# An attention-and-state-space kernel whose instruction order is planned: choosing the plan by replays, loading x's last block by column chunks, and moving two GpSimd steps

## The chip, the cores and the metric

The kernel runs on one NeuronCore of a Trainium2 chip. The metric is device time in microseconds (us) of one execution, as the median of several runs; lower is better. Engines in the text: PE (TensorE, matrix products), ACT (ScalarE), DVE (VectorE), POOL (GpSimd) and SP (SyncE, which here only issues DMAs).

## What is computed

Two independent halves, joined along the last axis: a state-space layer on `A_x` and multi-query attention on `B_x`, both with 2048 rows and 640 columns.

```python
def _A_ref(x, Lambda_re, Lambda_im, B_re, B_im, C_re, C_im, log_dt, Dskip):
    Lam_bar = exp(exp(log_dt) * Lam)                      # complex, 640 states
    Bu = einsum("bld,pd->blp", x, ((Lam_bar - 1) / Lam)[:, None] * Bmat)
    h[t] = Lam_bar * h[t-1] + Bu[t]                       # 2048 steps
    return 2 * einsum("blp,dp->bld", h, Cmat).real + x * Dskip

def _B_ref(x, wq, wk, wv, wo):                            # 32 heads of 20, one key and value head
    q, k, v = x @ wq, x @ wk, x @ wv
    p = softmax(q @ k.T * 20 ** -0.5)                     # 32 x 2048 x 2048
    return (p @ v).reshape(2048, 640) @ wo
```

## The kernel before

**Attention sets the length.** Scores are made transposed, in tiles of 128 keys by 512 queries: 4 blocks of queries x 8 groups of 4 heads x 16 key blocks x 4 heads = 2048 tiles. PE makes a tile (`score`, lines "SC<-QT,KT"); its exponential is taken either by ACT (`fill`, L1417: one ACTIVATE for two or three tiles of a PSUM slot, "PR<-SC") or by DVE, which forms the bits of a bf16 exponential by integer arithmetic (`fill_d`, L816, "BIG<-SC 128x512") and then needs three shifted copies of the result. POOL makes those copies two tiles at a time (`copy`, L1732, INT64_ADD) or DVE does (L816, "BIG<-BIG"). PE multiplies the exponentials with the values ("MB<-PR,VP" and, for DVE's tiles, four products each, "MB<-BIG,VS"), 32 query-head blocks one after the other, each ended by a copy of its PSUM bank (L1799, "pvsb"). There are two PSUM slots of three banks, SC0 and SC1, which ACT reads in turn.

**Beside it** PE, DVE and SP carry the rest as tasks: the projections of q (L1239, sent through DRAM as `qd` and brought back as `QT` by SP), the products of the state-space layer ("xaT", "CT,W", "CA,W"), the scaling of its matrices (`scale_b`, `scale_c`: L815, L816 and L811, "CA<-BA,sc", "W<-CT,sc"), the output projection.

**The prologue.** x (`B_x`) comes in four blocks of 512 rows. Blocks 0 and 1 are loaded as they lie and turned on PE (`turn`, with the identity `ident`, which DVE clears and POOL completes, L929); blocks 2 and 3 come through a transposing DMA (`loads`, L664): block 3 in two halves of 256 rows by 640 columns (`XB`). For each block `kv` (L1074 on) multiplies the five column chunks with `wkr` into one PSUM bank ("SC<-BIG,wkr"), takes the absolute maximum on DVE (L1087, `mab`) and writes the keys `KT` (L1093 on ACT; for block 1 on DVE). For block 3 it does so in two parts of 256 columns in the same bank. `bound` makes a bound from the maxima (L1113 to L1124: `Mp`, then `M0`), `qt_task` multiplies `M0` into the first query block, DVE writes it ("QT<-MB,lift"), and only then can the first score tile be made.

**What sets the order.** Each kernel instruction is an `Op` with an engine, a planned duration and dependences. `Schedule.run` plays a list-scheduling plan with those planned durations: on each engine, whenever it is free, `pick` takes the ready operation with the lowest `prio` whose `gate` holds. A DMA's planned landing comes from its bytes, its `issue` and `land` numbers, or from a fixed `lands`. `planned` (L509) makes 24 plans, the first with the task list as it stands and the others with due times moved by up to 12 tiles at random, and keeps the one with the earliest planned end. `Emitter.plan` then turns that plan into one fixed stream per engine with semaphore waits. On the chip each engine runs its stream in order: an instruction that waits holds all that is behind it. Waits are found per name: all columns of a PSUM bank carry one name, so a read of one half also waits for a write of the other half that stands ahead in the plan.

`keep_source` (L885) puts four 256-column products that change nothing ("MB<-KT,VZ", the left operand is zero) into PE's stream where the plan has had little matrix work in the last 3 us (`KEEP`).

## Time and profile before

| | us |
|---|---|
| median of 3 runs (all: 715.91, 712.63, 715.94) | 715.91 |
| the profiled execution | 715.61 |
| its span, first to last instruction | 713.9 |
| PE busy | 690.2 |
| ACT busy | 692.5 |
| DVE busy | 618.3 |
| POOL busy | 458.6 |
| first exponential of ACT starts | 20.35 |

The time outside the span (715.61 - 713.9 = 1.7 us) is launch and end. Times in the views are counted from the span's start. A row of a timeline gives the start, the length (of several merged instructions if "x" is above 1), the engine and the operation as output<-input; the bracket at its end is the idle time of the engine ahead of it and what ended it.

### The profile page before, as it was taken

The page shows a single profiled execution, that of the slowest core. Times are in us where ns is not written, and L with a number is a line of the kernel's source. Part 1 is how long each engine was busy: PE and PEld are TensorE (multiplying, and loading weights), DVE is VectorE, ACT ScalarE, POOL GpSimd, SP SyncE. Part 2 cuts the span into 40 slices and gives each one's busy share as a digit, 9 for nine tenths or more (in the row PEclk, how much of TensorE's full clock was granted, in tenths as well). Part 3 has the DMA queues.
Part 4 walks back from the last instruction along what each step waited for, and adds up shares of the span by engine and source line. Part 5 has one row for each costly group of instructions (what it writes and reads, how often), then busy time and mean ns, then how long its engine had stood idle before and what let it go on. Part 6 is the DMA issues. An engine that isn't in the chain of part 4 may idle for free.

```text
span 713.9 us, 26755 instructions
## 1 busy us (share of the span) xinstructions
PE 690.2 (97%) x11256; PEld 246.1 (34%) x11257; DVE 618.3 (87%) x1193; ACT 692.5 (97%) x700; POOL 458.6 (64%) x777
## 2 busy tenths in 40 slices
PE   7999989999999999999999999999999999999997
PEld 3322232343333433333433233334333333343323
DVE  7899869988998888788889999899999998877794
ACT  6899989999999999999999999999999999999996
POOL 3247745015688677565857867687767777868790
PEclk9999999999999999999999999999999999999999
DMA  9677642111111001101301001130000010110001
GB/s 187 171 176 165 141 92 67 45 30 25 32 45 31 13 19 25 48 16 30 65 7 39 19 11 39 34 68 15 13 19 20 11 25 26 27 38 18 25 14 40
DMA packets 77589, 34.44 MB, mean 48 GB/s; under 512 B 58350, under 2 KB 77470, under 8 KB 77470
## 3 DMA queue, kind: packets, MB, share of 16 engines
q1 hardware_dynamic: 76506, 32.44, 19.4%
q8 instruction: 90, 1.47, 0.9%
q10 hardware_dynamic: 964, 0.29, 0.2%
q14 instruction: 29, 0.24, 0.1%
HBM read 11.53 MB, written 9.75 MB: 30 GB/s over the span
## 4 chain that ended last, share of the span: by engine, by line
ACT 48%; PE 45%; SPq 2%; DMA 2%; DVE 2%; issue 1%; DVEq 0%
ACT PR L1417 48%; PE MB L679 17%; PE SC L679 11%; PE MB L749 11%; PE MB L759 4%; DMA CT<-in_A_C_im_dram 1%; SPq L664 1%; DMA BIG<-in_B_x_dram 1%; DVE BIG L816 1%; PE MB L675 1%; SPq L1851 1%; PE SC L749 0%; PE SC L675 0%; SPq L1291 0%; SPq L660 0%
## 5 line engine op out<-in xcount | busy, mean ns | idle before, releaser
L1417 ACT ACTIVATE PR<-SC 128x1024 bf16<-128x1024 f32 (+1 forms) x679 | 679.0, 1199 | 7.5 <-PE SC L679 5.2
L1732 POOL INT64_ADD BIG<-BIG x743 | 446.8, 618 | 224.9 <-DVE BIG L816 116.6
L816 DVE TENSOR_SCALAR BIG<-SC 128x512 int16<-128x512 f32 x531 | 357.3, 685 | 63.7 <-PE SC L679 58.2
L679 PE MATMUL SC<-QT,KT 32*128 32x512 bf16 x2014 | 266.1, 385 | 12.2 <-ACT PR L1417 5.8
L679 PE MATMUL MB<-BIG,VS 128*32 128x512 bf16 x2260 | 251.1, 384 | 0.5 <-DVE pvsb L1799 0.5
L679 PE MATMUL MB<-PR,VP 128*32 128x512 bf16 x1483 | 212.3, 384 | 0.4 <-DVE pvsb L1799 0.4
L679 PEld LDWEIGHTS SC<-QT,KT 32*128 32x128 bf16 x2014 | 67.8, 91 | 187.5 <-ACT PR L1417 125.0
L679 PEld LDWEIGHTS MB<-BIG,VS 128*32 128x32 bf16 x2260 | 60.1, 95 | 63.5 <-issue 41.9
L679 PEld LDWEIGHTS MB<-PR,VP 128*32 128x32 bf16 x1483 | 50.6, 94 | 48.9 <-issue 36.7
L749 PE MATMUL MB<-CT,W 128*32 128x320 bf16 (+2 forms) x1004 | 53.5, 301 | 0.2
L816 DVE TENSOR_SCALAR BIG<-BIG 128x1024 int16<-128x1024 int16 (+1 forms) x112 | 41.6, 404 | 2.8 <-PE MB L679 1.9
L749 PE MATMUL MB<-CA,W 128*32 128x512 bf16 (+1 forms) x640 | 35.4, 302 | 0.1
L759 PE MATMUL MB<-xaT,BT 32*128 32x256 bf16 x168 | 32.8, 275 | 1.1 <-ACT PR L1417 1.1
L749 PE MATMUL MB<-xaT,BA 128*32 128x256 bf16 x800 | 33.3, 280 | 0.6 <-DVE BIG L1239 0.6
L759 PE MATMUL MB<-diagD,xaT 32*128 32x128 bf16 x320 | 31.4, 217 | 0.0
L749 PEld LDWEIGHTS MB<-CT,W 128*32 128x32 bf16 x1004 | 22.8, 96 | 15.4 <-issue 6.8
L759 PEld LDWEIGHTS MB<-diagD,xaT 32*128 32x128 bf16 x320 | 17.7, 92 | 28.8 <-ACT PR L1417 20.9
L1984 DVE CAST stg<-MB 128x512 bf16<-128x512 f32 x35 | 23.8, 680 | 4.4 <-PE MB L749 3.6
L749 PE MATMUL MB<-xaT,BT 128*32 128x256 bf16 x632 | 26.6, 276 | 0.0
L811 DVE TENSOR_TENSOR prod<-MB,tab 128x1024 bf16<-128x1024 f32 x20 | 24.3, 1213 | 1.4 <-PE SC L679 1.0
L816 DVE TENSOR_SCALAR BIG<-MB 128x512 int16<-128x512 f32 x34 | 23.1, 679 | 0.0
L2251 DVE TENSOR_TENSOR_SCAN g<-sc,hst,prod 128x256 bf16<-128x256 f32 x30 | 22.9, 779 | 0.1
(168 smaller groups left out, 461.0 us busy)
## 6 DMA issues: line engine op xcount, KB each, us to landing
out_dram<-stg SPq DMA_DIRECT2D x31, 128.0 KB, 1.9
qd<-BIG SPq DMA_DIRECT2D x20, 128.0 KB, 2.2
QT<-qd SPq DMA_DIRECT2D x28, 80.0 KB
OP<-pvsb SPq DMA_DIRECT2D x105, 20.0 KB
rdP<-recs SPq DMA_DIRECT2D x105, 20.0 KB
lbd<-BA SPq DMA_DIRECT2D x5, 320.0 KB, 3.0
CT<-in_B_x_dram SPq DMA_DIRECT2D x2, 640.0 KB, 5.2
BA<-in_A_B_re_dram SPq DMA_DIRECT2D x1, 800.0 KB, 7.1
```

What stands on the lines that cost most here:

```text
L664: fns = [lambda e, o=o, i=i: e.dma_start_transpose(o, i) for o, i in pairs]
L675: r = e.matmul(out[32 * j:32 * j + 32], lhsT=lhsT[:, 32 * j:32 * j + 32], rhs=rhs, start=start, stop=stop, tile_position=(0, 32 * j), skip ...
L679: return lambda e: e.matmul(out, lhsT=lhsT, rhs=rhs, start=start, stop=stop, **kw)
L749: x = e.matmul(out[32 * j:32 * j + 32], lhsT=lhsT[:, 32 * j:32 * j + 32], rhs=rhs, start=start, stop=r.end is tag, tile_position=(0, 32 * ...
L759: return lambda e: e.matmul(out, lhsT=lhsT[at], rhs=rhs[at], start=False, stop=r.end is tag, tile_position=(32 * row, 0), skip_group_check ...
L811: return lambda e: e.tensor_tensor(out, a, b, op)
L816: return lambda e: e.tensor_scalar(out, a, s1, s2, op0=op0, op1=op1)
L1417: ex = self.act(lambda e: e.activation(dst, t[:, 0:512 * n], ACT.Exp, scale=1.0 / UNIT), 0.8333 * 512 * n + 64, table="exp", deps=[op], re ...
L1732: op.fns.append(lambda e: e.int64_add(words(dst), words(src), add))
L1851: fns = [lambda e, j=j, d=d, to=to, n=n, at=at: e.dma_start(p.OP[to:to + n, at, :], p.pvsb[32 * j + d:32 * j + d + n, slot, :]) for j, d, ...
L1984: ev = self.dve(lambda e: e.tensor_copy(st, bank.ap), 645, deps=[prev], reads=[bank.key], writes=[key], prio=self.EV, gate=(lambda: last.e ...
L2251: o = self.dve(lambda e, ri=ri, init=init: e.tensor_tensor_scan(p.g[:, u, ri, :], rdec, p.prod[:, 1, 0, ri, :], init, ALU.mult, ALU.add), ...
```

## The change

- `planned` makes 32 plans. Of each whose planned end lies within `MARGIN` of the best so far it also makes the streams, and `replay` runs those streams 12 times with other landing times for the DMAs (a mean and a spread for each kind, `FLIGHTS`, and now and then a late one). The plan with the lowest mean end is kept. `MARGIN = 2000.0` stands behind `planned`, but the class sets `MARGIN = 650.0` again further down (it did so before, for `fill_now`), so 650 ns is what counts.
- x's block 3 is transposed in two chunks of columns, 512 rows by 384 and 512 rows by 256. `kv` multiplies and reduces each block in one part of 512 columns, so `mab` has four maxima and `bound` one step less. All four `KT` are written by ACT.
- POOL's `ident` step has a lower `prio` number than its other constants, and POOL steps of more than 600 ns (that is the clearing of `VS`, 128x2048) wait in the plan until the first `mab` has started.
- Planned numbers change: `LANDS`, a table `LAND` of added flight time for DMAs (2500 ns for the transposes of B and C, `bt` and `ct`, in place of 1000 and 0; 1500 for `ba`; 2000 for `bn`), `KEEP` 3500 to 4200, `KEEP_Q` 4 in place of 12, `LATER` 5 in place of 7, 1850 for the clearing of `VS`.

```diff
-        for seed in range(self.PLANS):                     # PLANS = 24
+        for seed in range(self.PLANS):                     # PLANS, REPLAYS = 32, 12
...
-            end = max(op.end for op in plan.s.order) + self.COLD * self.quiet(plan.s.order)
+            cold = self.COLD * self.quiet(plan.s.order)
+            if best is not None and max(op.end for op in plan.s.order) + cold > best[0] + self.MARGIN:
+                continue
+            em = Emitter(self.nc, plan.s.order, [b.key for b in plan.banks], self.shared())
+            em.plan()
+            end = sum(em.replay(random.Random(k)) for k in range(self.REPLAYS)) / self.REPLAYS + cold
             if best is None or end < best[0]:
-                best = (end, plan)
+                best = (end, em)
...
+    def replay(self, rng):
+        S = Schedule
+        free, end = dict.fromkeys(S.ENGINES, 0.0), {}
+        for op in self.order:
+            e = op.eng
+            t = free[e]
+            for o in self.waits_of[id(op)]:
+                lag = S.OUT["dma"] if o.dma_key is not None else S.OWN.get(e, 0.0) if o.eng == e else S.OUT[o.eng]
+                t = max(t, end[id(o)] + lag)
+            if op.dma_key is not None:
+                free[e] = t + op.tail * len(op.fns)
+                if op.lands is not None:
+                    end[id(op)] = max(t + 1500.0, op.lands + abs(rng.gauss(0.0, 300.0)))
+                    continue
+                planned = op.end - op.start
+                mean, spread = self.FLIGHTS.get(op.dma_key.rstrip("0123456789"), (planned - 1000.0 * (planned > 3500.0), 500.0))
+                late = rng.gauss(mean, spread) + (rng.expovariate(1.0 / 1500.0) if rng.random() < 0.03 else 0.0)
+                end[id(op)] = t + max(1500.0, late)
+            else:
+                end[id(op)] = t + op.dur + op.tail
+                free[e] = t + op.dur - (S.EARLIER.get(e, 0.0) if op.psum else 0.0)
+        return max(end.values())
...
-    KEEP = 3500.0
+    KEEP, KEEP_Q = 4200.0, 4
...
-                                  prio=1 if eng == "pool" else 0.7, port=eng == "pool")
+                                  prio=(0.5 if name == "ident" else 1) if eng == "pool" else 0.7, port=eng == "pool",
+                                  gate=(lambda: 0 in self.red_op and self.red_op[0].start is not None) if dur > 600 and eng == "pool" else None)
...
-            o = self.loadT([(p.xbT[:, :, 512 * tb + lo:512 * tb + hi], xb[0, 512 * tb + lo:512 * tb + hi, :])], 800 * (hi - lo),
-                           f"xb{tb}{lo}", issue=6.0 * (hi - lo), writes=[f"xbT{tb}_{c}" + "h" * (lo > 0) for c in range(NC)])
+            o = self.loadT([(p.xbT[:, lo:hi, 512 * tb:512 * tb + 512], xb[0, 512 * tb:512 * tb + 512, 128 * lo:128 * hi])], 78000 * (hi - lo),
+                           f"xb{tb}{lo}", issue=600.0 * (hi - lo), writes=[f"xbT{tb}_{c}" for c in range(lo, hi)])
...
-    TURNED, KEYS = ("dadad", "dadad"), "adaa"
-    XB = ((2, 0, 512, 11100.0), (3, 0, 256, 12200.0), (3, 256, 512, 13100.0))
+    TURNED, KEYS = ("dadad", "dadad"), "aaaa"
+    XB = ((2, 0, 5, 11250.0), (3, 0, 3, 12500.0), (3, 3, 5, 13400.0))
+    LAND = dict(xa=1500.0, xa2=2000.0, bn=2000.0, bt=2500.0, ct=2500.0, ba=1500.0, pc=1200.0, qd=300.0)
...
-            parts = len(self.xb_op[tb, 0])
-            n = 512 // parts
-            for x in range(parts):
-                for c in range(NC):
-                    prev = self.pe(self.four(bank, [p.wkr[:, c, :]] * 4, p.xbT[:, c, 512 * tb + n * x:512 * tb + n * x + n],
-                                             c == 0, c == NC - 1, n * x, n), self.mmt(n), mode="C", prio=self.KP if tb < 3 else 1.15,
-                                   deps=[self.xb_op[tb, c][x], self.wk_op] + bank.last, prev=prev,
-                                   reads=[self.x_keys(tb, c)[x], "wkr"], writes=[bank.key])
-                red = self.dve(lambda e, src=bank.cols(n * x, n * x + n), at=tb + x: e.tensor_reduce(
-                    out=p.mab[:, at:at + 1], in_=src, axis=AX.X, op=ALU.max, apply_absolute_value=True), 115 + 1.05 * n, deps=[prev],
+            for c in range(NC):
+                prev = self.pe(self.four(bank, [p.wkr[:, c, :]] * 4, p.xbT[:, c, 512 * tb:512 * tb + 512], c == 0, c == NC - 1),
+                               self.mmt(512), mode="C", prio=self.KP if tb < 3 else 1.15,
+                               deps=[self.xb_op[tb, c], self.wk_op] + bank.last, prev=prev,
+                               reads=[f"xbT{tb}_{c}", "wkr"], writes=[bank.key])
+            red = self.dve(lambda e, src=bank.ap: e.tensor_reduce(out=p.mab[:, tb:tb + 1], in_=src, axis=AX.X, op=ALU.max,
+                                                     apply_absolute_value=True), 650, deps=[prev], reads=[bank.key],
...
-    EARLIER, LATER = 4, 7
+    EARLIER, LATER = 4, 5
```

Because the order is planned, nearly every stream changes. Counted in the streams of the two built kernels:

| | before | after |
|---|---|---|
| ACT exponentials of 1024 / 1536 / 512 columns | 554 / 125 / 0 | 557 / 123 / 1 |
| DVE exponentials (128x512) | 565 | 564 |
| shifted copies on DVE (one tile / two tiles) | 15 / 97 | 14 / 77 |
| shifted copies on POOL | 743 | 762 |
| zero products "MB<-KT,VZ" of 256 columns | 96 | 148 |
| DVE exponentials ahead of the first "W<-CT,sc" (L816; L862 in the new kernel) | 49 | 54 |
| products with the values that stand behind the last wait for an exponential of ACT | 13 | 4 |

More of the change, by code (lines that the diff above doesn't have):

```diff
@@ L114, in done @@
     def done(self, ops):
-        return all(o.end is not None and o.end + self.OUT.get(o.eng, 60.0) <= self.t for o in ops)
+        t = self.t
+        for o in ops:
+            if o.clear > t:
+                return False
+        return True
     def ready(self, op):
@@ L889, in keep_source @@
             return None
-        if self.pv_filled[b] == 64 and sum(len(q) for q in self.pvq[b]) < 12:
+        if self.pv_filled[b] == 64 and sum(len(q) for q in self.pvq[b]) < self.KEEP_Q:
             return None
@@ L1040, in xa_load @@
         self.xa_op[tb] = [self.loadT([(p.xaT[:, :, eo, lo:lo + 256], self.every(self.A_x[0, 512 * tb:512 * tb + 512, :], eo))], 327680,
-                                     f"xa{eo}", issue=1450.0, writes=[f"xaT{tb % 2}_{c}_{eo}" for c in range(NC)]) for eo in range(2)]
+                                     f"xa{eo}", issue=1450.0, land=self.LAND["xa2"], writes=[f"xaT{tb % 2}_{c}_{eo}" for c in range(NC)]) for eo in range(2)]
     @staticmethod
@@ L1074, in kv @@
         def kv(tb):
-            yield lambda: all((tb, c) in self.xb_op for c in range(NC)) and (tb < self.PLAIN or self.s.done(self.xb_op[tb, 0][:1])) \
+            yield lambda: all((tb, c) in self.xb_op for c in range(NC)) and (tb < self.PLAIN or self.s.done([self.xb_op[tb, 0]])) \
                 and any(x in self.early for x in self.free_banks)
@@ L1150, in v_task @@
                             for i in (2 * h, 2 * h + 1) for c in range(NC)], 10 * 28.0, mode="F", load=200.0,
-                           deps=[o for c in range(NC) for o in self.xb_op[tb, c]] + [self.wv_op] + bank.last, prev=prev, prio=3 if tb < 2 else 0.97,
-                           reads=[k for c in range(NC) for k in self.x_keys(tb, c)] + ["wvr"], writes=[bank.key],
+                           deps=[self.xb_op[tb, c] for c in range(NC)] + [self.wv_op] + bank.last, prev=prev, prio=3 if tb < 2 else 0.97,
+                           reads=[f"xbT{tb}_{c}" for c in range(NC)] + ["wvr"], writes=[bank.key],
                            gate=lambda: self.lively(self.V_BY[tb // 3]))
@@ L1184, with four @@
     started = False
-    def four(self, bank, lhs, rhs, start, stop, at=0, n=512):
-        return [self.mm(bank.tensor[32 * j:32 * j + lhs[j].shape[-1], bank.off + at:bank.off + at + n], lhs[j], rhs, start, stop,
+    def four(self, bank, lhs, rhs, start, stop):
+        return [self.mm(bank.tensor[32 * j:32 * j + lhs[j].shape[-1], bank.off:bank.off + 512], lhs[j], rhs, start, stop,
                         tile_position=(0, 32 * j), skip_group_check=True) for j in range(4)]
```

103 lines of the change are left out of this document (53 added, 50 removed).

## Prediction

> **What bounds the kernel now.** The page comes first: which engine is full, and which one the chain that ended last runs through.
>
> ```profile
> span 713.9 us, 26755 instructions
> PE 690.2 (97%) x11256; PEld 246.1 (34%) x11257; DVE 618.3 (87%) x1193; ACT 692.5 (97%) x700; POOL 458.6 (64%) x777
> ACT 48%; PE 45%; SPq 2%; DMA 2%; DVE 2%; issue 1%; DVEq 0%
> L1417 ACT ACTIVATE PR<-SC 128x1024 bf16<-128x1024 f32 (+1 forms) x679 | 679.0, 1199 | 7.5 <-PE SC L679 5.2
> ```
>
> ACT's 679 exponentials are busy for 679.0 us, 1.00 us each with their overlap. The timelines of ACT give their frame: start, last group, and the copy that follows them.
>
> ```profile
> 20.35 28.95 ACT L1417 ACTIVATE PR<-SC 128x1024 bf16<-128x1024 f32 x31 [1.58 <-PE SC L679]
> 689.59 15.60 ACT L1417 ACTIVATE PR<-SC 128x1024 bf16<-128x1024 f32 x14
> 706.34 0.60 ACT L1804 ACTIVATE pvsb<-MB 128x512 bf16<-128x512 f32 x1 [1.14 <-PE MB L679]
> ```
>
> They run from 20.35 to 689.59 + 15.60 = 705.19. So the profiled 715.61 us are a prologue of 20.35, 684.84 of exponentials of which 684.84 - 679.0 = 5.84 is idle, a tail of 713.9 - 705.19 = 8.7, and 1.7 outside the span. The profiled execution lies 0.3 below the median of 715.91. Whatever PE, DVE or POOL save counts only where it shortens one of these four pieces.
>
> Where are the 5.84? In one place, most of them:
>
> ```profile
> 100.19 1.02 ACT L1417 ACTIVATE PR<-SC 128x1024 bf16<-128x1024 f32 x1 [1.46 <-PE SC L679]
> 102.31 1.02 ACT L1417 ACTIVATE PR<-SC 128x1024 bf16<-128x1024 f32 x1 [1.10 <-PE SC L679]
> 103.84 1.02 ACT L1417 ACTIVATE PR<-SC 128x1024 bf16<-128x1024 f32 x1 [0.50 <-PE SC L679]
> 105.20 1.45 ACT L1417 ACTIVATE PR<-SC 128x1536 bf16<-128x1536 f32 x1 [0.33 <-PE SC L679]
> ```
>
> 1.46 + 1.10 + 0.50 + 0.33 = 3.39 us. The timelines of SP, DVE and PE, and the windows (length, then busy us and counts of PE, PEld, DVE, ACT and POOL, clock, DMA share, GB/s), say why:
>
> ```profile
> 66.78 3.69 SPq L664 DMA_TRANSPOSE CT<-in_A_C_re_dram  x1
> 91.58 3.28 SPq L664 DMA_TRANSPOSE CT<-in_A_C_im_dram  x1
> 91.84 0.68 DVE L816 TENSOR_SCALAR BIG<-SC 128x512 int16<-128x512 f32 x1
> 94.58 0.33 DVE L1840 RECIPROCAL rc<-dn 64x32 bf16<-64x32 bf16 x1
> 98.46 0.55 DVE L816 TENSOR_SCALAR W<-CT,sc 128x1280 bf16<-128x1280 bf16 x1 [3.54 <-DMA CT<-in_A_C_im_dram]
> 99.76 0.39 PE L679 MATMUL SC<-QT,KT 32*128 32x512 bf16 x3 [1.82 <-DVE BIG L816]
> 100.73 0.96 PE L749 MATMUL MB<-xaT,BA 128*32 128x256 bf16 x20 [0.57 <-DVE BIG L1239]
> 99.00:100.00 1.00, 0.24 (x3) 0.13 (x3) 1.00 (x4) 0.00 (x0) 0.00 (x0) 1.00 0.06 7
> 101.00:102.00 1.00, 1.00 (x25) 0.33 (x13) 1.00 (x3) 0.22 (x1) 0.95 (x2) 0.54 0.09 21
> 103.00:104.00 1.00, 1.00 (x17) 0.38 (x17) 0.17 (x2) 0.50 (x2) 0.59 (x2) 0.50 0.22 48
> ```
>
> DVE reaches the first step of `scale_c` at 94.92 and stands for 3.54 us, because the transposed C_im, issued at 91.58, lands only at 98.46. The DVE exponential behind it holds a PSUM slot, so PE cannot refill it (1.82 us idle), ACT runs dry (1.46), and right after that PE's granted clock is 0.50 for about three us, in which ACT loses the other 1.93. Everything is late because one DVE instruction stands too early in its stream.
>
> **The change, part by part.**
>
> *The C_im wait.* In the new streams the first `W<-CT` stands behind 54 DVE exponentials, not 49. The 49th is scored together with ACT's 74th exponential, the new 54th with ACT's 80th: 6 later at 1.00 us. The 49th ended at 92.52, so the new 54th ends about 92.5 + 6.0 - 0.6 (the shorter prologue, below) = 97.9, and `W<-CT` follows it at once. SP issues from 66.78 to 91.58 with pauses of 0.1 us or less; the new order has the same 25 issues there, in another order, and one `qd` store (0.45 us in the row below) less ahead of them. So C_im is issued at about 91.6 - 0.6 - 0.45 = 90.5 and lands 98.46 - 91.58 = 6.88 later, at 97.4, half a us before DVE asks.
>
> ```profile
> 83.77 0.45 SPq L1241 DMA_DIRECT2D qd<-BIG  x1
> ```
>
> That is thin. SP now has to pass the `brow` loads, which wait for a DVE step that stood behind the 35th DVE exponential and now stands behind the 43rd; by the same count it is done at about 85 us, when SP arrives. If SP waits up to 2 us there, DVE waits up to 1.5 at C_im. I take 0.5 us of wait left, with no fall of the clock: 3.39 - 0.5 = **2.9 us gained**; bounds 2.0 and 3.4.
>
> *x's block 3.* The rows of the prologue (PE, DVE), and the two sizes of the reduction by form:
>
> ```profile
> 16.12 0.40 PE L679 MATMUL SC<-BIG,wkr 128*32 128x256 bf16 x8 [0.56 <-DMA BIG<-in_B_x_dram]
> 16.58 0.42 DVE L1087 TENSOR_REDUCE mab<-SC 128x1 f32<-128x256 f32 x1 [2.26 <-PE SC L679]
> 17.06 0.51 PE L679 MATMUL SC<-BIG,wkr 128*32 128x256 bf16 x12 [0.53 <-DVE mab L1087]
> 17.62 0.42 DVE L1087 TENSOR_REDUCE mab<-SC 128x1 f32<-128x256 f32 x1 [0.23 <-PE SC L679]
> 18.16 0.35 DVE L1121 SCALAR_TENSOR_TENSOR M<-mask,mab,Mp 128x128 bf16<-128x128 f32 x1
> 18.60 0.40 PE L679 MATMUL MB<-BIG,M 128*32 128x512 bf16 x4
> L1087 DVE TENSOR_REDUCE mab<-SC 128x1 f32<-128x512 f32 x3 | 2.0, 683 | 0.0
> 707.10 0.60 PE L675 MATMUL SC<-WO,OP 128*32 128x512 bf16 x8
> ```
>
> The last half lands at 16.08 (PE starts 0.04 later). Its products are cut in two by the first half's reduction: that stands behind 8 of them because the bank has one name, and the other 12 stand behind it. From landing to the `M0` product: 18.60 - 16.08 = 2.52 us. In the new order 12 products wait for the first chunk and 8 of 512 columns (0.60, a row of that shape from the tail) for the second; then one reduction of 683 ns and `M0`: 0.04 + 0.60 + 0.02 + 0.68 + 0.12 (end of the reduction to `M0`: 18.16 - 18.04) + 0.44 (`M0` to its product) = 1.90, **0.6 gained**. The `wvr` products between stay under it: 40 in 1.17 us behind one dummy product end 1.85 after the landing. The landing itself is unknown, as no chunk of this shape is in the trace. The bytes are the same and the last piece is two fifths of the block instead of half; as the two halves landed 1.3 us apart (PE's starts 14.84 and 16.12), I allow 0.6 either way: 0 to 1.2 gained, and take 0.6.
>
> *Identity first, `VS` later.* The scalars' chain starts sooner, but ACT then waits for `mab` anyway. The clearing of `VS` moves behind POOL's last `fr` step, which ended at 12.14, and DVE's `VS` steps wait for it ahead of block 2's reduction:
>
> ```profile
> 1.94 1.80 POOL L958 MEMSET VS<- 128x2048 bf16 x1
> 11.37 0.77 POOL L2066 INT64_ADD fr<-fr  x2 [3.03 <-DVE fr L816]
> ```
>
> At the latest it ends at 12.14 + 1.80 = 13.9, and the reduction behind it at 14.7: DVE then stood idle until 16.58. Nothing, as long as x's block lands last.
>
> *ACT's work.* By form:
>
> ```profile
> L1417 ACT ACTIVATE PR<-SC 128x1024 bf16<-128x1024 f32 x554 | 520.2, 1115 | 6.2 <-PE SC L679 4.9 <-PE MB L679 1.0
> L1417 ACT ACTIVATE PR<-SC 128x1536 bf16<-128x1536 f32 x125 | 177.2, 1572 | 1.2 <-PE MB L679 0.9 <-PE SC L679 0.3
> ```
>
> 3 x 520.2/554 - 2 x 177.2/125 + 0.6 (one of 512 columns; ACT's copy of that size at 706.34 took 0.60) = 2.82 - 2.84 + 0.6: **0.6 lost**. DVE's 21 copies fewer (20 are doubles) and POOL's 19 more lie beside it: neither is full.
>
> *The tail.* Behind the last exponential 13 products with the values had to run before the copy at 706.34, 1.14 us later; the new order leaves 4, one step of PE instead of three to four, at 0.2 us each: **0.5 gained**, bounds -0.3 and 0.6.
>
> *What the new plan does elsewhere* can't be read from counts: the other 5.84 - 3.39 = 2.45 us of ACT's idle time may be 1 to 4.5. I leave it.
>
> **Sum:** 715.61 - 2.9 - 0.6 - 0.5 + 0.6 = **712.2 us**.
>
> **The rivals.**
>
> *The wait stays, or one like it takes its place.* Replays choose among plans, but only among those within 650 ns of the best planned end, and planned landings are guesses. For it: C_im's margin above is half a us. Against: DVE asks 3 us later than before. Time: 715.61 - 0.6 - 0.5 + 0.6 = 715.1. Chance 0.20.
>
> By the Trainium skill, "TensorE: Matmul & The Clock Gate", section "HAM oscillation — how this bites in real kernels", only PE gaps above some 3.4 us lower the clock; such a wait would then cost ACT the 1.46 alone, and the time be 713.2. This trace speaks against it: gaps of 1.82 and 0.57 us were enough. I give it 0.03 of those 0.20.
>
> *Slower: SP's queue.* Should DVE come late to `brow` or to the cast whose store SP issues ahead of C_im, C_im is late by as much. The other terms save 0.5, so it is slower than before from a wait of 3.54 + 0.5 = 4.0 us on, that is, with C_im landing after 101.9, 4.5 later than my count; with 6 us of wait, at 3.39/3.54 each, 715.1 + 2.4 = 717.5. Chance 0.07.
>
> *The zero products.* 13 more groups of four stand in PE's stream.
>
> ```profile
> L679 PE MATMUL MB<-KT,VZ 128*32 128x256 bf16 x96 | 4.9, 273 | 0.0
> ```
>
> If each holds back a score that ACT waits for, 13 x 0.27 = 3.5 us: 715.7. Against: PE is idle for 713.9 - 690.2 = 23.7 us, and they are planned into idle stretches. Chance 0.05.
>
> *Better:* the chunk lands earlier and the other idle time halves: 712.2 - 0.6 - 1.2 = 710.4 or less. Chance 0.08.
>
> **How the numbers follow.** Forecast 0.60, the rivals 0.20, 0.07, 0.05 and 0.08. A measurement of this kernel tells about 0.5% from no change, 3.6 us: faster means under 712.3 against the median of 715.91. The forecast lies on that edge, and I put 57% of its 0.60 below it: 0.34; with the better case 0.42. Slower by over 0.5% (above 719.5) needs the SP case at its worst; with what I have not seen in a new order, 0.07. Same 0.51. The range runs from 709.9, most of the better case, to 716.0, which takes in the case where the wait stays and the zero products, and leaves out the slower one.
>
> **What would show it.** Right: the first `W<-CT` waits for C_im for under 1 us; no window near 100 us has a clock under 1; the first exponential starts near 19.7; ACT's idle time between first and last exponential is near 3; the last copy comes about 0.6 after the last exponential. Wrong: a single DVE or PE wait for a DMA of over 2 us with ACT idle behind it, wherever it is; a first exponential after 20.4.

## The result and the profile after

The changed kernel takes 711.47 us in the median of 13 runs (709.37 to 713.6), the kernel before, run beside it, 713.27 us (712.48 to 716.23). The ratio is 0.9964, 95% interval 0.9946 to 0.9981: 0.4% faster, which is inside the 0.5% that the prediction called no change (it gave that case 0.51). The forecast was 712.2. Its range, 709.9 to 716.0, also holds the 713.27 of before, so that the time lies inside it says little; the rows have to show whether the reasons were right.

The profiled execution took 711.06 us against 715.61, so 4.55 less where the forecast said 3.4. The page of the changed kernel, in the same lines as those of before:

```profile
span 709.2 us, 26838 instructions
PE 688.4 (97%) x11287; PEld 246.0 (35%) x11287; DVE 610.4 (86%) x1168; ACT 693.6 (98%) x703; POOL 467.3 (66%) x796
L1457 ACT ACTIVATE PR<-SC 128x1024 bf16<-128x1024 f32 (+1 forms) x681 | 679.4, 1197 | 4.0 <-PE SC L725 2.8
```

ACT still bounds it. The frame of its exponentials comes from ACT's timeline of the changed kernel (start, length, then in brackets the idle time before and who ended it):

```profile
19.15 12.94 ACT L1457 ACTIVATE PR<-SC 128x1024 bf16<-128x1024 f32 x14 [1.53 <-PE SC L725]
33.32 667.73 ACT L1457 ACTIVATE PR<-SC 128x1024 bf16<-128x1024 f32 x667 [1.23 <-PE SC L725]
701.71 0.60 ACT L1844 ACTIVATE pvsb<-MB 128x512 bf16<-128x512 f32 x1 [0.66 <-PE MB L725]
```

The prologue is 19.15 (20.35 before), the exponentials last until 33.32 + 667.73 = 701.05, that is 681.90 (684.84 before) with 679.4 of work, and the tail is 709.2 - 701.05 = 8.15 (8.7 before). 1.20 + 2.94 + 0.55 make the 4.7 by which the span is shorter. Near 100 us ACT no longer stops. DVE, SP and the windows of the changed kernel there:

```profile
97.85 0.55 DVE L862 TENSOR_SCALAR W<-CT,sc 128x1280 bf16<-128x1280 bf16 x1 [0.56 <-DMA CT<-in_A_C_im_dram]
```

```profile
91.09 3.40 SPq L710 DMA_TRANSPOSE CT<-in_A_C_im_dram  x1
```

```profile
99.00:100.00 1.00, 0.64 (x11) 0.12 (x8) 1.00 (x3) 1.00 (x2) 1.00 (x2) 1.00 0.12 27
101.00:102.00 1.00, 1.00 (x21) 0.24 (x17) 0.86 (x3) 1.00 (x2) 0.44 (x1) 1.00 0.43 140
103.00:104.00 1.00, 1.00 (x18) 0.32 (x15) 1.00 (x3) 0.94 (x2) 0.57 (x1) 1.00 0.25 53
```

DVE waits 0.56 us for C_im where it waited 3.54, ACT's column reads 1.00 and 0.94 where it read 0.00 to 0.50, and the clock stays at 1.00.

One thing does not fit: the profiled executions differ by 4.55 us, the medians by 1.8. Before's 13 runs lie in two groups, eight from 712.48 to 713.75 and five from 714.88 to 716.23, and the profiled 715.61, an execution beside those 13, lies with the upper. The experiments have to say what the groups are.

### The profile page after: what moved, and what is told of

Its sections match the earlier page's. It is cut to its first block, busy times and chain, and to the rows that moved or that the text cites. A ratio compares the mean times of both kernels' runs of the same rounds, so it can differ in the third digit from the quotient of the medians.

```text
span 709.2 us, 26838 instructions
## 1 busy us (share of the span) xinstructions
PE 688.4 (97%) x11287; PEld 246.0 (35%) x11287; DVE 610.4 (86%) x1168; ACT 693.6 (98%) x703; POOL 467.3 (66%) x796
## 4 chain that ended last, share of the span: by engine, by line
ACT 49%; PE 44%; DMA 3%; DVE 2%; SPq 1%; issue 0%; DVEq 0%
ACT PR L1457 49%; PE MB L725 17%; PE MB L795 11%; PE SC L725 11%; PE MB L805 4%; DMA mrep<-mab 2%; SPq L710 1%; DMA BIG<-in_B_x_dram 1%; DVE BIG L862 1%; PE MB L721 1%; DMA mcol<-mrep 1%; PE SC L721 0%; DMA qd<-BIG 0%; SPq L706 0%; DVE prod L857 0%
## 5 line engine op out<-in xcount | busy, mean ns | idle before, releaser
L1457 ACT ACTIVATE PR<-SC 128x1024 bf16<-128x1024 f32 (+1 forms) x681 | 679.4, 1197 | 4.0 <-PE SC L725 2.8
L1772 POOL INT64_ADD BIG<-BIG x762 | 455.4, 614 | 214.3 <-DVE BIG L862 118.7
L862 DVE TENSOR_SCALAR BIG<-SC 128x512 int16<-128x512 f32 x529 | 356.3, 685 | 67.7 <-PE SC L725 60.8
L725 PE MATMUL MB<-BIG,VS 128*32 128x512 bf16 x2256 | 247.8, 384 | 0.3 <-DVE pvsb L1839 0.2
L725 PE MATMUL MB<-PR,VP 128*32 128x512 bf16 x1484 | 204.9, 384 | 0.0
L805 PE MATMUL MB<-xaT,BT 32*128 32x256 bf16 x184 | 35.6, 272 | 1.6 <-ACT PR L1457 1.4
L862 DVE TENSOR_SCALAR BIG<-BIG 128x1024 int16<-128x1024 int16 (+1 forms) x91 | 34.7, 410 | 2.6 <-PE MB L725 2.3
L862 DVE TENSOR_SCALAR BIG<-MB 128x512 int16<-128x512 f32 x35 | 23.8, 680 | 0.0
L795 PE MATMUL MB<-WO,OP 128*32 128x128 bf16 (+1 forms) x480 | 23.5, 302 | 0.0
```

The lines of the kernel that those rows point to most:

```text
L725: return lambda e: e.matmul(out, lhsT=lhsT, rhs=rhs, start=start, stop=stop, **kw)
L795: x = e.matmul(out[32 * j:32 * j + 32], lhsT=lhsT[:, 32 * j:32 * j + 32], rhs=rhs, start=start, stop=r.end is tag, tile_position=(0, 32 * ...
L805: return lambda e: e.matmul(out, lhsT=lhsT[at], rhs=rhs[at], start=False, stop=r.end is tag, tile_position=(32 * row, 0), skip_group_check ...
L862: return lambda e: e.tensor_scalar(out, a, s1, s2, op0=op0, op1=op1)
L1457: ex = self.act(lambda e: e.activation(dst, t[:, 0:512 * n], ACT.Exp, scale=1.0 / UNIT), 0.8333 * 512 * n + 64, table="exp", deps=[op], re ...
L1772: op.fns.append(lambda e: e.int64_add(words(dst), words(src), add))
```

## The experiments

Each kernel below keeps every stream of its parent as the planner wrote it, unless a line says otherwise; a function `moved` takes an instruction out of the finished order and puts it back elsewhere, and the waits are then worked out anew. Where a ratio is given, it stands on 12 runs of the kernel and 29 to 35 of before on the same chip. These runs lie on three chips, of which the changed kernel ran on one (the chip of the result's runs is not on record), so a comparison of two ratios is often one across chips. Each run comes with its mean granted clock, which turned out to carry much of the answer; a run at 0.999 or above is called one at full clock.

**Before, with C_im issued early.**

```diff
+    ct = [o for o in order if o.dma_key in ("ct0", "ct1")]
+    order.remove(ct[1])
+    order.insert(order.index(ct[0]) + 1, ct[1])
```

> Before's streams, unchanged but for one issue: SP issues the transpose of C_im directly behind that of C_re (about 70 us instead of 91.58). Theory A (the prediction's: before loses 3.39 us of ACT's idle time to the wait of W<-CT for C_im): the first W<-CT doesn't wait for a DMA, the clock stays at 1.00 near 100 us, ACT's idle time falls from 5.84 to about 2.5, and the time falls by about 3.4 against an execution of before that has the wait (715.6 to 712.2). Since before's 13 runs lie at 712.5 to 713.8 (eight of them) and at 714.9 to 716.2 (five), A also says that the wait costs its full 3 us only in the upper group: the five runs of this kernel should all lie below 713.5. Rival B (the spread of before's runs has another cause, and the wait costs in every run): the median falls by 3 us or more against before's median, to 710, and its runs still lie in two groups 2 to 3 us apart. Rival C (something that waits behind the earlier transpose, 3.3 us of SP's queue near 70 us, stalls in its place): a new DMA wait of 1 to 3 us between 70 and 91 us, and no gain.

Measured: median 713.34 (711.77 to 717.85), before 713.02 (710.75 to 718.82), ratio 0.9986 (0.9961 to 1.0012). The profiled execution took 711.77, and its rows (DVE; then ACT) show half of what theory A said:

```profile
86.70 0.29 DVE L822 TENSOR_SCALAR BIG<-BIG 128x512 int16<-128x512 int16 x1 [1.67 <-DMA qd<-BIG]
95.89 0.45 DVE L823 TENSOR_SCALAR W<-CT,sc 128x1280 bf16<-128x1280 bf16 x1
```

```profile
82.12 199.15 ACT L1424 ACTIVATE PR<-SC 128x1024 bf16<-128x1024 f32 x190 [0.17 <-PE MB L686]
```

`W<-CT` waits for nothing and ACT runs through 100 us. But there is a new wait of 1.67 for a `qd` store, as rival C had it; in this execution it cost ACT nothing. The runs show no gain either, as C said. A's claim on them failed: it had all below 713.5, and five of the 12 were above, one at 717.85 with a clock of 0.993. At full clock the median was 713.3 against 712.3 of before, so taking the wait away by itself did not make the kernel faster. The one trace is the fastest of the 12 runs and doesn't say where that 1 us lies.

**Before, with the reduction of the first half ahead.**

```diff
+    red = next(o for o in order if o.writes == ["mab3"])
+    second = next(o for o in order if o.eng == "pe" and "wkr" in o.reads
+                  and any(k.endswith("h") for k in o.reads))
+    order.remove(red)
+    order.insert(order.index(second), red)
```

> Before's streams, with the reduction of the first half of x's block 3 ordered ahead of the second half's products. By the prediction's reading, 12 of the second half's products are held up by that reduction and its row order. If so, the stretch from the landing of the last half to the M0 product falls from 2.52 us to about 1.9 or less without any chunks by columns, the first exponential from 20.35 to about 19.7, and the time by 0.6 us, provided the landing stays at 16.08. Rival: the landing itself is what moved (the profiled change has it at 15.49), so that the order is worth nothing: then the stretch stays at about 2.5 and the first exponential at 20.35. Whole time: within 0.7 us of before's either way.

Measured: median 712.22 (710.82 to 713.29), ratio 0.9976 (0.9956 to 0.9997). PE's prologue in this kernel, and then in the changed one:

```profile
15.70 0.73 PE L687 MATMUL SC<-BIG,wkr 128*32 128x256 bf16 x20 [0.64 <-DMA BIG<-in_B_x_dram]
17.46 0.40 PE L687 MATMUL MB<-BIG,M 128*32 128x512 bf16 x4
```

```profile
15.53 0.62 PE L725 MATMUL SC<-BIG,wkr 128*32 128x512 bf16 x8 [0.36 <-DMA BIG<-in_B_x_dram]
17.40 0.40 PE L725 MATMUL MB<-BIG,M 128*32 128x512 bf16 x4
```

The 20 products of the half run in one piece (0.73 where before they took 0.40 and, after a pause, 0.51). From PE's start on the last piece to the `M0` product it is 1.76 us here, 1.87 in the changed kernel and 2.48 before. These stretches came out equal, within 0.02, in all further traces that show the last piece by itself: 2.47 to 2.48 in four more with before's order, 1.76 in one more with the reduction ahead, 1.86 to 1.87 in four more with chunks. So in this stretch the order is the whole of it, and the chunks by columns are 0.11 worse than halves in a good order.

In the runs this gain can't be told from noise: at full clock the median is 712.23 against 712.32 of before. The ratio comes from something else. None of the 12 runs was under 0.999, against 13 of 35 of before, and why is open.

The trace holds a second find, in DVE's and ACT's rows of the same kernel:

```profile
96.42 0.55 DVE L824 TENSOR_SCALAR W<-CT,sc 128x1280 bf16<-128x1280 bf16 x1 [2.63 <-DMA CT<-in_A_C_im_dram]
```

```profile
98.15 1.02 ACT L1425 ACTIVATE PR<-SC 128x1024 bf16<-128x1024 f32 x1 [0.55 <-PE SC L687]
99.82 181.92 ACT L1425 ACTIVATE PR<-SC 128x1024 bf16<-128x1024 f32 x173 [0.65 <-PE SC L687]
```

The wait for C_im is there, 2.63 us long, and costs ACT 0.55 + 0.65 = 1.20, not 3.39: no window between the first and the last exponential has a clock under 1. PE stood for 0.91 and 0.57 us there.

**After, with C_im issued later.**

```diff
+    im = next(o for o in order if o.dma_key == "ct1")
+    sp = [o for o in order if o.eng == "sp"]
+    third = sp[sp.index(im) + 3]
+    order.remove(im)
+    order.insert(order.index(third) + 1, im)
```

> After's streams, with SP's issue of C_im put behind the next three issues (1.38, 0.54 and 0.44 us): issued at about 93.5 instead of 91.09, landing at about 100.3, so the first W<-CT waits for about 3.1 us instead of 0.56. By the prediction's price (3.39 us of ACT per 3.54 us of wait, with the clock at 0.50 for some three us behind it) the time rises by about 2.4 to 3, to about 714. By the rule that only gaps above 3.4 us lower the clock, it rises by about 1.2 (1.46 of 3.39 per 3.54), to about 712.7, and the clock near 103 us stays at 1.00. If PE or ACT have work ahead there, it rises by nothing.

Measured: median 712.73 (711.56 to 714.94), ratio to before 0.9982 (0.9959 to 1.0005). DVE, PE, ACT and the windows of the profiled execution (712.70):

```profile
98.50 0.55 DVE L873 TENSOR_SCALAR W<-CT,sc 128x1280 bf16<-128x1280 bf16 x1 [2.67 <-DMA CT<-in_A_C_im_dram]
```

```profile
100.50 0.62 PE L806 MATMUL MB<-BIG 128*32 128x512 bf16 x4 [2.36 <-DVE BIG L1290]
```

```profile
101.70 1.02 ACT L1468 ACTIVATE PR<-SC 128x1024 bf16<-128x1024 f32 x1 [2.08 <-PE SC L736]
103.93 598.84 ACT L1468 ACTIVATE PR<-SC 128x1024 bf16<-128x1024 f32 x597 [1.20 <-PE SC L736]
```

```profile
100.00:101.00 1.00, 0.50 (x4) 0.11 (x4) 0.91 (x2) 0.00 (x0) 1.00 (x2) 0.60 0.47 147
101.00:102.00 1.00, 1.00 (x14) 0.25 (x14) 0.29 (x1) 0.29 (x1) 0.96 (x2) 0.50 0.49 51
102.00:103.00 1.00, 1.00 (x16) 0.30 (x8) 1.00 (x3) 0.73 (x1) 0.00 (x0) 0.50 0.50 163
103.00:104.00 1.00, 1.00 (x15) 0.23 (x11) 0.07 (x1) 0.07 (x1) 0.61 (x1) 0.69 0.11 25
```

A wait of 2.67 us, as long as the one above, costs ACT 2.08 + 1.20 = 3.28: PE stood for 2.36 us, the clock fell, and the stretch of 0.40 + 0.50 + 0.50 + 0.31 = 1.71 us of lost clock is one of 3.42 us at 0.50. So the price of such a wait is not a slope. It is a small part, 0.8 to 1.2 us where the clock held (the rows above and below, all in before's streams), and here, where it fell, an estimated 2 us on top: 3.28 less 1.20, as if the small part were the same in these streams. Six of the 12 runs had a clock under 0.999; their median is 713.7, that of the others 712.0. The expected 714 was missed: the wait came out shorter (2.67 where 3.1 was expected), and the fall did not come in every run.

**After's code with the old choice of the plan.**

```diff
-    PLANS, REPLAYS = 32, 12
+    PLANS, REPLAYS = 24, 12
-            end = sum(em.replay(random.Random(k)) for k in range(self.REPLAYS)) / self.REPLAYS + cold
+            end = max(op.end for op in plan.s.order) + cold
```

> After's whole code, but the plan chosen as before chose it: 24 plans instead of 32, by the planned end alone, no replays. That picks another seed (5) with new streams. Theory A (most of the gain comes from the chunks, the landing margins and the retuned constants, and the choice among plans is worth under 1 us): 711 to 712.5. Rival D (the selection of the plan is the gain; a plan chosen the old way has a wait like C_im's somewhere): 713.5 to 716, with a DMA wait of over 1 us on DVE or PE and ACT idle behind it. The new margins make planned landings later, so A is likelier: I expect 712.

This kernel has a plan of its own. Measured: median 710.70 (708.96 to 713.62), ratio 0.9960 (0.9937 to 0.9982), beside the changed kernel's 0.9964 (0.9946 to 0.9981). Its profiled execution took 709.05, with ACT's exponentials in one row, 680.11 us for 679.3 of work:

```profile
19.09 680.11 ACT L1457 ACTIVATE PR<-SC 128x1024 bf16<-128x1024 f32 x681 [1.45 <-PE SC L725]
```

The longest wait of DVE or PE for a DMA after 20 us is 0.68, at 130.05 for a `qd` store, and ACT runs on through it. Rival D fell: for this one pair of plans the choice by replays brought nothing that shows beside the width of the two intervals, and theory A's value was 1.3 too high.

**Before with two hand moves.** The reduction as above, and C_im and the `dn` load ahead of the five `OP` stores in SP's queue.

```diff
...
+    im = next(o for o in order if o.dma_key == "ct1")
+    sp = [o for o in order if o.eng == "sp"]
+    dn = sp[sp.index(im) - 1]
+    at = sp.index(dn)
+    while any(k.startswith("OP") for k in sp[at - 1].writes):
+        at -= 1
+    for o in (im, dn):
+        order.remove(o)
+        order.insert(order.index(sp[at]), o)
```

> Before's streams with two hand moves and nothing else: the reduction of the first half of x's block 3 ahead of the second half's products, and on SP C_im (and the dn load) ahead of the five OP stores, so that C_im is issued near 87.5 instead of 91.58 and lands near 94.3, under a us before DVE asks for it at about 94. Theory A (these two waits are nearly the whole gain of the change): no W<-CT wait above 0.5 us, first exponential near 19.3, mean of the runs at 711.5 to 712, that is within 0.5 us of the changed kernel's 711.4, and fewer runs with a clock under 0.999 than before's 13 of 35. Rival E (the rest of the new plan is worth more than a us): the mean stays above 712.5. Rival C (the stores pushed back by 3.3 us make a wait of their own): a new DVE wait of 1 us or more for qd or dn, mean above 713.

Measured: median 711.80 (710.58 to 717.08), mean 712.3, before 714.94 (711.22 to 722.07), ratio 0.9952 (0.992 to 0.9984). C_im was issued at 85.30, DVE waited for no DMA after 20 us, the first exponential came at 19.54, and two of the 12 runs were under a clock of 0.999, against 17 of 29 of before. C fell, and the mean lies between A and E, 0.3 above A's range. At full clock the median is 711.5 against 712.5, so 1.0 of the gain is there in every run, and the rest of the ratio is falls of the clock that these runs did not have. The changed kernel gained 2.3 at full clock on another chip (below), so E's point, that the rest of the new plan is worth something too, is not ruled out.

**After with two hand moves.** C_im is put ahead of the two `OP` stores, and DVE's `Mm` step eight instructions later. For the latter, DVE's rows of the changed kernel, and SP's:

```profile
32.14 0.33 DVE L857 TENSOR_TENSOR Mm<-maskM,mcol 128x160 bf16<-128x160 f32 x1 [1.64 <-DMA mcol<-mrep]
```

```profile
17.38 0.32 SPq L705 DMA_DIRECT2D mrep<-mab  x1
...
28.33 0.36 SPq L705 DMA_DIRECT2D mcol<-mrep  x1
```

This wait is the 1.23 of ACT at 33.32 that the result showed.

```diff
...
+    mm = next(o for o in order if o.writes == ["Mm"])
+    dve = [o for o in order if o.eng == "dve"]
+    other = dve[dve.index(mm) + 8]
+    order.remove(mm)
+    order.insert(order.index(other) + 1, mm)
```

> After's streams with two hand moves: DVE's Mm step eight DVE instructions later (it waited 1.64 us for mcol at 32.14 and ACT lost 1.23 behind it), and C_im ahead of the two OP stores on SP (issued near 89.5 instead of 91.09). If the two remaining waits of the profile are what is left to win, the profiled idle time of ACT falls from 2.5 to about 1 us, the median from 711.5 to about 710.2, and the upper runs (713.4 to 713.6) go. If the run-to-run spread is made elsewhere, the median stays at 711 to 711.5.

Measured: median 710.16 (709.27 to 715.44), before 714.94, ratio 0.9945 (0.9912 to 0.9978). The median is as expected, but four runs were under a clock of 0.999, the profiled one (711.47) among them. Its DVE row, PE rows and windows near 70 us:

```profile
68.88 0.29 DVE L879 TENSOR_SCALAR BIG<-BIG 128x512 int16<-128x512 int16 x1 [0.81 <-DMA qd<-BIG]
```

```profile
68.64 0.39 PE L743 MATMUL SC<-QT,KT 32*128 32x512 bf16 x3 [0.39 <-ACT PR L1475]
...
69.83 0.39 PE L743 MATMUL SC<-QT,KT 32*128 32x512 bf16 x3 [0.46 <-DVE BIG L880]
70.52 0.39 PE L743 MATMUL SC<-QT,KT 32*128 32x512 bf16 x3 [0.30 <-DVE BIG L880]
```

```profile
68.00:69.00 1.00, 0.61 (x11) 0.17 (x8) 0.19 (x2) 1.00 (x2) 0.00 (x0) 1.00 0.49 95
69.00:70.00 1.00, 0.54 (x11) 0.16 (x7) 1.00 (x3) 1.00 (x2) 0.73 (x2) 1.00 1.27 290
70.00:71.00 1.00, 0.61 (x6) 0.13 (x3) 1.00 (x3) 1.00 (x2) 1.00 (x2) 1.00 1.28 291
71.00:72.00 1.00, 0.98 (x16) 0.46 (x16) 1.00 (x2) 1.00 (x2) 1.00 (x3) 0.59 0.52 150
```

No pause of PE here is longer than 0.46 us, and the clock falls all the same, behind three us in which PE was busy for 0.54 to 0.61 of the time. Ahead of them DVE waited 0.81 us for a `qd` store, and PE then waited twice for DVE's exponentials.

**After without the zero products.** All groups that `keep_source` had put in are left out; they add zeros to sums. The expectation below speaks of 109 groups; the traces count 148 products (11287 matrix products in the changed kernel, 11139 here), which is 37 groups of four.

```diff
+    order[:] = [o for o in order if not (o.eng == "pe" and o.prio == 8 and "VZ" in o.reads)]
```

> After's streams without the products with the zero matrix VZ (109 groups of four); they add zeros, and the output is the same. By the rival with the zero products, each group that stands ahead of a score costs up to 0.27 us, and the time falls by up to 3 us. By the forecast they lie in PE's idle stretches: within 0.5 us of 711.4. A third way: PE's idle stretches without them let the clock fall; then more runs show a clock below 0.999 than after's 2 of 13, and the time rises by a us or more.

Measured: median 714.66 (710.84 to 719.53), ratio to before 0.9987 (0.9955 to 1.0019). Six of 12 runs under 0.999, the lowest 0.988. The profiled execution (714.5) shows one fall; the windows of this kernel, where the changed one ran `MB<-KT,VZ` products:

```profile
134.00:135.00 1.00, 0.14 (x5) 0.00 (x0) 1.00 (x5) 1.00 (x2) 0.00 (x0) 1.00 0.03 8
135.00:136.00 1.00, 0.72 (x9) 0.21 (x9) 0.49 (x3) 1.00 (x3) 0.00 (x0) 1.00 0.00 0
136.00:137.00 1.00, 0.57 (x7) 0.21 (x10) 1.00 (x2) 1.00 (x2) 0.00 (x0) 0.95 0.00 0
137.00:138.00 1.00, 1.00 (x13) 0.32 (x6) 1.00 (x3) 1.00 (x2) 0.00 (x0) 0.50 0.00 0
```

The time did not fall by 3 us, so the rival of the prediction had the wrong sign. The third way is the likeliest of the three, but not shown: this interval overlaps the changed kernel's, which did not run on this chip. Beside it on this chip ran the changed kernel with two hand moves (above): 709.8 at full clock against 712.9 here, a difference of which the moves account for 0.7 on another chip. Nor is the clock all of it: this difference stands at full clock. In the profiled execution the fall costs ACT 0.47, while it loses 0.98, 0.69 and 0.51 us at 350, 490 and 631 us, where the changed kernel has no such stops and runs no zero product either (its last starts at 229). The first stands behind PE's wait of 1.11 us for a load of `xaT`; for the other two the trace names no cause.

**Before again, twice.** Two more executions of the unchanged kernel.

> The kernel before, unchanged, for one more look at where its executions differ. Expected: C_im's landing is 6 to 7 us behind an issue near 91; where DVE's wait for it is above about 3 us the clock falls behind it (profiled execution 0.998), where it is below 2.6 us it doesn't (1.000), and the two differ by about 2 us.

> The kernel before, unchanged, for one more trace, in the hope of one of its executions at 0.993 or below (9 of 29 and 8 of 35 runs). Expected there: three or more stretches of 3.4 us at half clock, each behind a stretch in which PE was busy for less than half of some 3 us; where they lie is open.

They took 712.67 and 712.26 us, both at a clock of 1.000. DVE and ACT of the first:

```profile
96.65 0.55 DVE L817 TENSOR_SCALAR W<-CT,sc 128x1280 bf16<-128x1280 bf16 x1 [2.27 <-DMA CT<-in_A_C_im_dram]
```

```profile
98.38 1.02 ACT L1418 ACTIVATE PR<-SC 128x1024 bf16<-128x1024 f32 x1 [0.18 <-PE SC L680]
100.06 181.90 ACT L1418 ACTIVATE PR<-SC 128x1024 bf16<-128x1024 f32 x173 [0.65 <-PE SC L680]
```

The wait is there in both (2.27 and 2.34 us) and costs ACT 0.83 and 0.90, with no fall of the clock, as expected for waits below 2.6 us. An execution at 0.993 was not caught.

**Before with its C_im wait kept warm.** Six more groups of zero products stand ahead of the scores that wait (`near` is the planned group closest in time, `at` the place of those scores in the order).

```diff
...
+    order[at:at] = [copy.copy(near) for _ in range(6)]
```

> Before's streams, with six more groups of four products with the zero matrix (about 0.25 us each) in PE's stream directly ahead of the scores that stand behind DVE's wait for C_im. The wait itself is left as it is. Theory A (the 3.39 us have two parts: about 1.5 us of missing scores and about 2 us of half clock after the PE gap): the wait of W<-CT stays at 2.3 to 3.5 us, PE's gap there falls under 1 us, the clock stays at 1.00 from 101 to 105 us, and ACT's idle time there is 1 to 1.6 us. Runs with a clock of 0.997 to 0.998 become rarer, and the mean falls by 0.5 to 1 us against before's on the same chip. Rival F (the clock falls for another reason than PE's idle share): it falls all the same. If runs at 0.993 and below stay as frequent as in before, those have their stalls elsewhere.

Measured: median 713.80 (712.22 to 720.74), ratio 1.002 (0.9987 to 1.0054). PE and DVE of the profiled execution (712.45):

```profile
97.42 0.83 PE L690 MATMUL MB<-KT,VZ 128*32 128x256 bf16 x24
```

```profile
96.48 0.55 DVE L827 TENSOR_SCALAR W<-CT,sc 128x1280 bf16<-128x1280 bf16 x1 [1.91 <-DMA CT<-in_A_C_im_dram]
```

The gap is filled, and ACT loses 0.22 + 0.25 = 0.47 behind it, but the wait of this execution was short, so it proves little. No run had 0.997 or 0.998, and five had 0.991 to 0.993: the expectation that the mean falls was missed. Before on this chip had two of 29 at 0.997 and six below, so the test had hardly any single falls to remove. Runs at 0.993 and below did not become rarer, which by the expectation means that they have their stalls elsewhere; no trace shows where.

**The changed kernel again, and the better one beside it.**

> The changed kernel, unchanged, beside the next runs on one chip. Theory A (the change's gain in the mean is about 1.4 us at full clock, and the rest that fewer executions lose clock time): at clocks of 0.999 and above 711.1 against 712.4 of before; all runs together 711.4 against 714 to 715; fewer than 3 in 10 runs under 0.999, where before had 13 in 35 and 17 in 29. Rival (the clock's falls hit both alike on a given chip): as many runs under 0.999 as before, and a difference of medians of 1.4 us.

> The two hand moves on after's streams (Mm later on DVE, C_im ahead of two stores on SP) once more, beside the changed kernel on the same chip: 1 us less than it at clocks of 0.999 and above (710.1 against 711.1); in the median of all runs 0.5 to 1.3 us less. If the difference is under 0.3 us, the earlier 710.16 was the chip.

On one chip: before 713.03 (710.75 to 719.33), the changed kernel 711.19 (709.67 to 715.26), ratio 0.9968 (0.9937 to 0.9999); the better one 709.70 (709.18 to 710.18), ratio 0.9944 (0.9925 to 0.9964). At full clock the medians are 712.7, 710.4 and 709.7. Theory A had fewer than 3 in 10 of the changed kernel's runs under 0.999; it was four of 12, beside eight of 29 of before. So on this chip the rival was right about the falls: they hit both alike.

This chip gives the cleanest pair of traces, both at a clock of 1.000: before at 712.26 (its span is 710.5) and the changed kernel at 710.10 (708.4). ACT's rows of before (the first, one from the middle, the last), then of the changed kernel:

```profile
19.50 29.25 ACT L1418 ACTIVATE PR<-SC 128x1024 bf16<-128x1024 f32 x31 [1.58 <-PE SC L680]
49.56 10.61 ACT L1418 ACTIVATE PR<-SC 128x1024 bf16<-128x1024 f32 x11 [0.82 <-PE MB L680]
593.95 107.89 ACT L1418 ACTIVATE PR<-SC 128x1536 bf16<-128x1536 f32 x109 [0.41 <-PE MB L680]
```

```profile
19.15 12.94 ACT L1458 ACTIVATE PR<-SC 128x1024 bf16<-128x1024 f32 x14 [1.54 <-PE SC L726]
32.51 309.06 ACT L1458 ACTIVATE PR<-SC 128x1024 bf16<-128x1024 f32 x301 [0.42 <-PE SC L726]
341.79 358.39 ACT L1458 ACTIVATE PR<-SC 128x1024 bf16<-128x1024 f32 x366 [0.22 <-PE SC L726]
```

The prologue is shorter by 0.35, the exponentials by 1.31 (682.34 to 681.03), the tail by 0.44 (8.66 to 8.22): 2.10 in all. ACT's idle time within the exponentials falls from 3.54 to 1.73, for 0.5 more work. Of before's 3.54, the wait for C_im made 0.90 and the stop at 49.56 made 0.82. That stop, of 0.81 or 0.82 us, is in all seven traces of before's streams and in none of the new ones.

ACT's row of the better one:

```profile
19.07 680.48 ACT L1476 ACTIVATE PR<-SC 128x1024 bf16<-128x1024 f32 x681 [1.54 <-PE SC L744]
```

With 679.2 us of work, 1.3 of ACT's idle time is left, where the changed kernel had 1.7 here and 2.5 in its first trace. None of its 12 runs lost the clock here; on the other chip four did. It is 0.56% faster than before, and in the medians 1.5 us faster than the changed kernel, 0.7 at full clock where 1 was expected, though the two intervals against before overlap.

## Why the prediction was right, point by point

| term | predicted (bounds as gains) | profiled pair | what the runs showed |
| --- | --- | --- | --- |
| C_im wait | -2.9 (2.0 to 3.4) | -3.4 | the wait costs 0.8 to 1.2 where the clock held, 3.4 where it fell |
| x's block 3 | -0.6 (0 to 1.2) | -1.20 | -0.61 from the order, the rest is the landing |
| tail | -0.5 (-0.3 to 0.6) | -0.55 | the copy came 0.66 after the last exponential, not 1.14 |
| ACT's work | +0.6 | +0.4 | 679.4 against 679.0 |
| rest | 0 | +0.1 | a new stall of 1.23 at `Mm`; before's stop of 0.82 near 50 us is gone, and smaller ones |

*The time and the gain.* The time came out as forecast (712.2, measured 711.47), the gain did not: 3.4 was forecast, and the medians differ by 1.8. The forecast started from an execution of before with a fall of the clock and took the cost of that fall away again, so its time does not depend on how often before has such a fall; its gain does. In the profiled execution, 711.06, the time is 1.1 below the forecast: the landing of x's block 3 gave 0.6 more and the C_im wait 0.5 more than was taken.

*The C_im wait.* The count of DVE's place and of SP's issues held: issue at 91.09 (predicted 90.5), 0.56 us of wait (predicted 0.5), no fall of the clock. What the prediction took for one price are two. The wait costs 0.83, 0.90 and 1.20 us at 2.27, 2.34 and 2.63 us while the clock holds. Where it falls, as in the profiled execution of before, an estimated 1.9 to 2.1 us come on top. The forecast was set against that execution alone, and so holds for it (3.4 gained where 2.9 was forecast). At full clock the traces put this term at about 0.9. The runs do not confirm that figure by itself: with the wait taken away and nothing else changed, they were not faster (713.3 against 712.3).

*The two groups of before's runs* are probably this clock: of those 13 runs no clocks are on record, and the profiled 715.61 had 0.998. In every fall between the first and the last exponential for which there is a trace (four) the windows add up to one stretch of 3.42 us at 0.50, which is 0.0024 of the run's mean clock; by that estimate 0.997 or 0.998 is one stretch and 0.993 three. Over the three chips 38 of before's 93 runs were under 0.999, of the changed kernel's 25 runs six, counted in the two comparisons; runs at 0.997 to 0.998 of before lie some 2 to 3 us above those at 0.999 and up. What the change gains in every run is 2.3 us at full clock, where both ran on one chip (712.7 against 710.4). That it also makes falls rarer is not shown: on that chip it was four of 12 runs against eight of 29. Where the three and more stretches of a run at 0.993 lie is open: no trace caught one.

*x's block 3.* The stretch was predicted at 1.90 from the landing and came out at 1.91 (17.40 - 15.49). The other 0.6 of the profiled pair is the landing, and that is not the chunks: PE started on the last half at 15.08 to 16.12 in seven traces, mean 15.67; on the last chunk, in five traces that show it, at 15.45 to 15.87, mean 15.57. The prediction allowed 0.6 for it and was right to take none.

*The tail* and *ACT's work* were mis-sized by 0.2 us at most in the profiled pair.

*The rest* was set to nothing and was nothing only in sum: DVE's `Mm` step waits 1.64 us for `mcol` and costs 1.23 of ACT, while before's 0.82 near 50 us is gone. That they nearly cancel is chance: in the second trace of the changed kernel the `Mm` wait is 1.16 and costs 0.42. Moving it and C_im gave 0.7 us at full clock. It was visible in before's streams as an order, not as a wait, in the one execution that was read; two of the later ones have it (0.61 and 0.45 us).

*The rivals.* The wait did not stay. By the Trainium skill, "TensorE: Matmul & The Clock Gate", section "HAM oscillation — how this bites in real kernels", the rule is to have no idle gaps of PE above some 3.4 us, and the prediction took that to mean that only such gaps lower the clock. Here the clock fell behind gaps of 1.82 and 0.57, behind one of 2.36, and behind three of 0.30 to 0.46 us, so the 0.03 that the prediction gave this rule was enough. SP was not late. The zero products did not cost 3 us: without them the ratio to before is 0.9987 (0.9955 to 1.0019), with them, on other chips, 0.9964 and 0.9968. That they save time is likely, and not shown. None of the prediction's signs of being wrong came: the longest wait of DVE or PE for a DMA in the profiled execution, from the first exponential on, is the 1.64 at `Mm`.

*What the change's own words claim.* In the one case tried, the replays chose a plan no better than the old rule did (0.9964 against 0.9960). Chunks are no better than halves in the right order. Two hand moves in before's streams, one of them a single reduction, give 0.9952, but at full clock only 1.0 us of the changed kernel's 2.3, on another chip. The tail and the stop near 50 us, which these moves leave as they were, fit the difference.

## What to carry to other kernels

Read more than one execution before pricing a wait: one that makes PE idle has a small price that it always has, and a step, here about 2 us, that it has only where the clock falls behind it. Compare the two kernels in executions in which the clock held. Where two parts of one block share a bank, look at the order of the reader of the first part and the writers of the second before cutting the block differently. Look for short DVE steps that wait for a DMA round trip and stand ahead of work that frees banks; here, moving one of them and one DMA issue a few places gave 0.7 us, where another way of choosing among whole plans gave nothing that could be measured.

## What the hardware showed that was not expected

- A fall of the clock lasts 3.42 us at 0.50 each time (before, and three of the experiments). What it cost ACT differed: 1.93 in before, about 2.1 with C_im late, 1.04 in the fall at 71 us, 0.5 in the one at 137 us; what decides it was not tried. PE's busy share alone doesn't tell when it comes: three us at 0.54 to 0.61 did it in one trace, while the changed kernel's two us around 32 us, in which PE waited for 1.50 us, did not.
- Chunks of different shape landed at the same time: mean 15.67 for the last half, 15.57 for the last two fifths.
- A store of `mrep` (2.5 KB) issued at 17.38 let `mcol` go only at 28.33, 10.95 us later, with the loads of B issued from 13.79 to 14.88 ahead of it in the same queue. The second of these landed at 28.15. In all 13 traces that give its landing, `mcol` started after it, by 0.2 to 1.1 us in twelve and 2.1 us in one. That fits loads that hold up the store behind them; it was not tried.
